# A Fourier filter and gated convolution on one core: taps over two blocks at once, transfers on one queue and in pieces, short products on zeros, and a new order of the work

## The chip, the cores and the metric

One NeuronCore of a Trainium2 chip runs the whole program. It has a matrix engine (PE, TensorE, with its weight loads shown apart as PEld), a vector engine (DVE), a scalar or activation engine (ACT), GpSimd (POOL) and a queue engine (SP, SyncE) that here only issues transfers. ACT can issue transfers as well. Data lie in HBM, in the on-chip SBUF of 128 partitions, and in PSUM, into which PE writes.

The metric is the time of one execution on the device in microseconds, from the median of several runs. A profile is of one execution; its span goes from its first to its last instruction.

## What is computed

The input x has 8 batches of 3200 positions and 256 channels. Per batch it is Fourier transformed along the positions, the spectrum is mixed by a complex 256 x 256 matrix with a bias, shrunk by 0.01 towards zero, and transformed back. On the result y a gate is formed from a causal convolution of five taps for each channel, multiplied with a 256 x 256 product of y, and multiplied by one more matrix.

```python
X = np.fft.rfft(x, axis=1)
Yr = Xr @ w_r - Xi @ w_i + b_r
Yi = Xr @ w_i + Xi @ w_r + b_i
Yr = np.sign(Yr) * np.maximum(np.abs(Yr) - lam, 0.0)      # Yi likewise, lam = 0.01
y = np.fft.irfft(Y, n=x.shape[1], axis=1)
...
for k in range(K):                                         # K = 5
    gate_pre += conv_w[k][None, None, :] * xp[:, k:k + S, :]
gate = 1.0 / (1.0 + np.exp(-gate_pre))
return (gate * (y @ w_val) @ w_out).astype(np.float32)
```

## The kernel before

3200 positions are split as 64 x 50, so that each transform is two stages of small matrix products. The stages of one batch are these:

- `p1`, units u = 0 to 7: load a unit of x (two halves of 50 rows, `load`), its products on PE (L553 to L560), a copy of one half of the result by ACT (L566), sum and difference on DVE (`fold`, L572), and a store of both to a scratch tensor `a_dram` in HBM (L514 by `by_rows`; the first unit has four odd stores of 25 rows, L592).
- `p2`, slices d = 0 to 6: load a slice of `a_dram` (L613), second transform on PE (L631), splitting of the result in a high and a low part on ACT and DVE (L672 to L684), mixing (`mixed`: `mix_sum` L749, bias on DVE L751, `mix` L745, shrinking L757 and L759), first inverse transform (L700), store to `z_dram` (L716).
- `positions`, blocks k = 0 to 7: load of `z_dram` (L800), second inverse transform (L811), copy to `y_sb` (L815). A block is 400 positions.
- `gated`, the same blocks: first product of the gate on ACT (`first`, L872), the four other taps on DVE (`tap`, L875), sigmoid on ACT (L885), the matrix product `v_ps` (L845, in the last batches L841), the gate on DVE (L887), a split in two parts (L348, L350), the matrix product `o_ps`, its copy (L912) and the stores of the output (L914). All of `first`, `tap` and sigmoid run per block and per half of the channels, over 400 elements in 128 partitions.

Matrices `w_val`, `w_out` and the taps arrive as 64-bit floats; `from_float64` turns one into 32-bit numbers by thirteen steps on DVE (L390, L396).

Several batches are under way at once. What is written in the program is not an order but pieces: each is given to `plan.add` with an engine, a due time `at`, its cost, and the tiles it uses and sets. `Plan.order` walks through a made timeline and, on each engine, takes of the pieces that can begin soonest the one with the smallest `at`; the numbers in the table `O` shift the due times of kinds of pieces. The engines then get their instructions in that order and work through them strictly in turn, waiting for tiles by semaphores. A tile of a pool with n buffers can be opened only when the one n before it has been read for the last time: PSUM has three buffers `ps_2` (for nearly everything) and two `ps_y` (for the mixing).

In batch 0 the halves of x and of the stores are spread over two queues, SP and ACT (`QUEUES`). For the first two batches loads of x and stores to `a_dram` are cut in pieces of 48 and 2 rows (`ROWS`); later they go as 50 rows. PE multiplies a tile of zeros between the early units (`warm`, L939), 8 of these products ahead of batch 1.

Of the kernel before, what the change touches and what calls it, by code (L numbers as in the profile page):

```python
# [10 lines left out]
F32 = mybir.dt.float32  # L11
# [10 lines left out]
NH = 2  # L22
# [82 lines left out]
class Plan:  # L105
# [30 lines left out]
    def order(self):  # L136
# [41 lines left out]
        while len(done) < len(pieces):  # L178
# [32 lines left out]
            p["start"], p["end"] = start, end  # L211
# [30 lines left out]
WIRE = 230  # L242
# [8 lines left out]
def act(n, kind="copy"):  # L251
# [9 lines left out]
O = {'spread': -43.2582,  # L261
     'hold': 0.1723,
     'together': 1.3472,
     'later': 16.9988,
     'load_x': -1.6525,
     'p1': -3.0866,
     'p1_step': 1.6595,
     'load_a': -5.4475,
     's2': -2.5217,
     's1i': 1.3927,  # L270
     'p3': 3.8457,
     'load_z': -27.5528,
     'y': 14.5177,
     'conv': 12.9924,
     'val': 3.2379,
     'gate': -21.5703,
     'project': 5.6082,
     'late_val': 6.023,
     'late_out': 14.484,
     'turn': -27.2503,  # L280
     'pre': 6.946,
     'mix_sum': -2.1531,
     'p1_1': -2.5925,
     'load_x_1': -0.3328,
     'p1_2': 0.3179,
     'p3_0': -1.1611}
# [9 lines left out]
def fourier_filter_then_gated_conv(ctx: ExitStack, tc: tile.TileContext, x, w_r, w_i, b_r, b_i,  # L296
# [224 lines left out]
    QUEUES = (("SP", nc.sync), ("ACT", nc.scalar))  # L521

    def p1(b, u, at):
# [55 lines left out]
        def store(h):  # L579
            if u == 0 and h in (0, None):  # L580
                buffer(ka, "a_dram", [Q, NM * D])
            dst = tl[ka].rearrange("(h f) mc -> f h mc", h=NH)
            hs = slice(0, NH) if h is None else slice(h, h + 1)
            eng = QUEUES[h][1] if early else nc.sync
            for k in range(2):
                lo = u * 4 * D + k * 512
                n = D if lo == 0 else 0
                by_rows(eng, dst[:, hs, lo + n:lo + 512], st()[k * HP:k * HP + N2, hs, n:], rows)
            if u == 0:
                for g in range(NH) if h is None else (h,):  # L590
                    for r in range(2):
                        eng.dma_start(out=dst[r::2, g, 0:D], in_=st()[r:N2:2, 1 - g if r else g, 0:D])  # L592
        for h in range(NH) if early else (None,):
            key = ("a_dram", b, (u, h))
            A_KEYS.setdefault(b, []).append(key)
            if early:
                STORED.append(("stored", 0, (u, h)))
            uses = [ks + (1,)] if h == 0 and u else [ks + (0,)] if h == 1 and u else [ks + (0,), ks + (1,)]
            add(at + 0.02, QUEUES[h][0] if early else "SP", 1300 if early else 1500, lambda h=h: store(h), uses,
                [key] + ([STORED[-1]] if early else []), {ka: "a_dram"} if u == 0 and not h else None, kb=200 if early else 400)  # L600
# [166 lines left out]
    AHEAD = 2  # L767
# [25 lines left out]
    def positions(b, k, at):  # L793
# [7 lines left out]
        add(at + O["load_z"], "SP", 400, load, [("z_dram", b, u) for u in range(NU)], [kz + (0,)], {kz: "zl"}, kb=400, chain="zl")  # L801
# [45 lines left out]

    def gated(b, k, at):
        bk = (b, k)
        here, there = y_keys(k, 0), [key for key in y_keys(k, 1) if key not in y_keys(k, 0)]  # L850
        ky, kg, kv, kh, kp, ko = (("y_hl", bk), ("acc", bk), ("v_ps", bk), ("gated", bk), ("o_ps", bk), ("o", bk))
# [14 lines left out]
        acc = lambda c: tl[kg][:, c, :]  # L866

        def first(c):
            if c == 0:
                buffer(kg, "acc", [P, 2 * TB])  # L870
                tl[kg] = tl[kg].rearrange("p (c n) -> p c n", c=2)
            nc.scalar.mul(block(acc(c)), y_at(k, c, 0), cw_sb[:, c, 0:1])  # L872

        def tap(c, j):
            nc.vector.scalar_tensor_tensor(out=block(acc(c)), in0=y_at(k, c, j), scalar=cw_sb[:, c, j:j + 1],  # L875
                                           in1=block(acc(c)), op0=ALU.mult, op1=ALU.add)
        for c in range(2):
            add(at + O["conv"] + 0.01 * c, "ACT", act(TB, "conv"), lambda c=c: first(c), [*here, *there, ("cw", 0, 0)],
                [kg + (c,)], {kg: "acc"} if c == 0 else None, chain="conv")
        for j in range(1, KC):  # L880
            for c in range(2):
                add(at + O["conv"] + 0.02 * j, "DVE", 61 + dve(TB), lambda c=c, j=j: tap(c, j), [*here, *there], [kg + (c,)],
                    delay=545 + (130 if j == KC - 1 else 0))
        for c in range(2):
            add(at + O["conv"] + 0.15, "ACT", act(TB, "sigmoid"), lambda c=c: nc.scalar.activation(  # L885
                out=acc(c), in_=acc(c), func=AF.Sigmoid), (), [kg + (c,)])
        add(at + O["gate"], "DVE", dve(2 * TB), lambda: nc.vector.tensor_tensor(  # L887
            out=tl[kg], in0=tl[kv][:, :, 0:TB], in1=tl[kg], op=ALU.mult), [kv + (0,), kv + (1,)], [kg + (0,), kg + (1,)])
        if bk in LATE_OUT:
            gs = [kg + (0,), ("w_late", 0, 0)]  # L890
            om = lambda e: matrix(kp, e, lambda: w_late[1], lambda h, c: tl[kg][:, c, :], True)
        else:
            gs = [*split(at + O["gate"] + 0.1, 2 * TB, kh, lambda: tl[kg], lambda: tl[kh][:, 0], lambda: tl[kh][:, 1],
                         [kg + (0,)], {kh: "g_hl"}, lambda: buffer(kh, "g_hl", [P, 2, 2, TB], F32R)),
# [38 lines left out]

    def warm(v, n):
# [5 lines left out]
    add(-200, "POOL", 100, lambda: nc.gpsimd.memset(nlam, -LAM), (), [("nlam", 0, 0)])  # L940

# [31 lines left out]
    for b in range(B):  # L973
# [13 lines left out]
        for k in range(NB + AHEAD):  # L987
            if k < NB:
                positions(b, k, start + (k - AHEAD) * T / NB)
            if k >= AHEAD:  # L990
                gated(b, k - AHEAD, start + (k - AHEAD) * T / NB)
    plan.run(tc)
# [25 lines left out]
```

## Time and profile before

| | |
|---|---|
| median of three runs | 868.22 us (866.73 to 869.12) |
| the profiled execution | 869.32 us, of which its span is 867.5 |
| PE busy | 825.7 us, 95% of the span |
| DVE busy | 768.2 us, 89% |
| ACT busy | 612.6 us, 71% |
| chain that ended last | PE 61%, DVE 16%, DMA 11%, ACT 6% |
| moved by DMA | 162.25 MB, mean 187 GB/s |

In what follows, L and a number is a line of the program before unless it is said to be of the changed one. A busy share is a mean over stages that have different limits; the tables by stage give busy time of each engine in a stretch with the number of its instructions, the TensorE clock that was granted (1.00 is full), the mean busy share of the 16 DMA engines, and GB/s. In a row of the timeline an idle time in brackets is that of the engine just before it, and what ended it. Rows of a long matrix product count each record of the profiler, of which a 32-bit product has two.

### The profile page before, as it was taken

What the parts mean: (1) busy time and instruction counts of PE and PEld (TensorE: products, weight loads), DVE (VectorE), ACT (ScalarE), POOL (GpSimd) and SP (SyncE); (2) the same over time, 40 slices, a digit from 0 to 9 for tenths busy, and PEclk for the clock granted to TensorE, in tenths of its full rate; (3) what the DMA queues carried; (4) which work ended last, traced back from release to release, by engine and by line L of the source; (5) the groups of instructions that cost most, each with busy time, mean ns of one, the idle gap of its engine ahead of it and who ended that gap; (6) DMA issues with size and microseconds to landing.
All of it is one profiled execution on the core that took longest, in us unless ns stands there. A gap on an engine that the chain in (4) does not pass through costs nothing.

```text
span 867.5 us, 23798 instructions
## 1 busy us (share of the span) xinstructions
PE 825.7 (95%) x9814; PEld 696.1 (80%) x9814; DVE 768.2 (89%) x1262; ACT 612.6 (71%) x1030; POOL 6.2 (1%) x11
## 2 busy tenths in 40 slices
PE   6888967999999999999999999999999999999997
PEld 2346755888888888898888898898888999998774
DVE  2526678799999999999999999999999999999996
ACT  1225645788877778787787778877787887776673
POOL 0000000000000000000000000000020000000000
PEclk7578989999999999999999999999999999999999
DMA  6679777768775668557675768557674557324422
GB/s 167 177 175 241 242 190 216 223 204 237 237 225 163 202 197 243 182 167 201 198 235 198 222 195 241 179 170 200 199 237 159 151 150 196 109 84 163 153 70 82
DMA packets 123973, 162.25 MB, mean 187 GB/s; under 512 B 10592, under 2 KB 98298, under 8 KB 123866
## 3 DMA queue, kind: packets, MB, share of 16 engines
q1 hardware_dynamic: 122106, 157.47, 61.3%
q10 hardware_dynamic: 1760, 3.28, 1.5%
q8 instruction: 77, 1.26, 0.6%
q14 instruction: 30, 0.25, 0.1%
HBM read 82.06 MB, written 78.64 MB: 185 GB/s over the span
## 4 chain that ended last, share of the span: by engine, by line
PE 61%; DVE 16%; DMA 11%; ACT 6%; issue 2%; SPq 2%; ACTq 0%; DVEq 0%
PE o_ps L845 12%; PE y_ps L745 11%; PE v_ps L845 10%; PE y_p L811 8%; PE y_ps L749 6%; DVE acc L875 5%; PE z_ps L700 4%; PE s L631 4%; DMA x<-in_x 3%; PE p L553 3%; DMA a<-a_dram 3%; DMA a_dram<-s 3%; DVE s L572 2%; DMA f_sb<-in_f 1%; DVE tp L759 1%
## 5 line engine op out<-in xcount | busy, mean ns | idle before, releaser
L875 DVE SCALAR_TENSOR_TENSOR acc<-y_sb,cw_sb,acc 128x400 f32<-128x400 f32 x512 | 301.5, 627 | 6.1 <-ACT acc L872 4.8
L745 PE MATMUL y_ps<-w_sb,xs 128*128 128x256 f32 x1152 | 156.9, 286 | 11.7 <-DVE y_ps L751 11.7
L745 PEld LDWEIGHTS y_ps<-w_sb,xs 128*128 128x128 f32 x1152 | 144.8, 190 | 22.3 <-DVE y_ps L751 13.7
L845 PE MATMUL o_ps<-gated,wo_sb 128*128 128x400 f32 x744 | 151.4, 349 | 0.7 <-DVE xs L680 0.4
L845 PEld LDWEIGHTS o_ps<-gated,wo_sb 128*128 128x128 f32 x744 | 132.4, 188 | 8.2 <-issue 2.5
L845 PE MATMUL v_ps<-y_hl,wv_sb 128*128 128x400 f32 x648 | 130.0, 347 | 1.4 <-ACT o L912 0.6
L572 DVE TENSOR_TENSOR s<-p,s 128x512 f32<-128x512 f32 (+2 forms) x144 | 89.9, 626 | 37.7 <-ACT s L568 22.6
L845 PEld LDWEIGHTS v_ps<-y_hl,wv_sb 128*128 128x128 f32 x648 | 115.5, 188 | 3.6 <-issue 1.3
L811 PEld LDWEIGHTS y_p<-g_sb,zl 100*64 100x64 f32 x2048 | 89.3, 137 | 26.0 <-issue 4.9
L811 PE MATMUL y_p<-g_sb,zl 100*64 100x100 f32 x2048 | 99.6, 252 | 0.5 <-issue 0.2
L749 PE MATMUL y_ps<-w_sb,xs 128*128 128x256 f32 x576 | 88.5, 292 | 6.0 <-ACT y_ps L727 5.5
L749 PEld LDWEIGHTS y_ps<-w_sb,xs 128*128 128x128 f32 x576 | 78.5, 193 | 16.0 <-ACT y_ps L727 11.3
L757 ACT ACTIVATE tp<-y_ps,nlam 128x512 f32<-128x512 f32 (+1 forms) x104 | 69.5, 672 | 24.3 <-PE y_ps L745 22.2
L872 ACT ACTIVATE acc<-y_sb,cw_sb 128x400 f32<-128x400 f32 x128 | 77.2, 630 | 12.0 <-DVE gated L350 11.9
L553 PE MATMUL p<-x,f_sb 50*64 50x512 f32 x256 | 71.2, 639 | 9.0 <-issue 6.3
L348 ACT CAST gated<-acc 128x800 fp32r<-128x800 f32 x62 | 53.4, 861 | 31.4 <-DVE acc L887 31.2
L759 DVE SCALAR_TENSOR_TENSOR tp<-y_ps,tp 128x512 f32<-128x512 f32 (+1 forms) x104 | 68.6, 663 | 5.8 <-ACT tp L757 5.4
L885 ACT ACTIVATE acc<-acc 128x400 f32<-128x400 f32 x128 | 66.9, 539 | 8.6 <-DVE acc L875 8.3
L560 PE MATMUL p<-x,f_sb 50*64 50x512 f32 x240 | 71.9, 646 | 0.0
L727 ACT COPY y_ps<-bias_sb 128x256 f32<-128x256 f32 x104 | 39.7, 382 | 45.5 <-DVE tp L759 38.5
L348 ACT CAST y_hl<-y_sb 128x800 fp32r<-128x800 f32 x54 | 46.5, 860 | 28.5 <-PE v_ps L845 26.5
L631 PEld LDWEIGHTS s<-f_sb,a 64*64 64x64 f32 x3072 | 52.1, 138 | 15.9 <-issue 6.8
(84 smaller groups left out, 1029.3 us busy)
## 6 DMA issues: line engine op xcount, KB each, us to landing
zl<-z_dram SPq DMA_DIRECT2D x64, 400.0 KB
out<-o SPq DMA_DIRECT2D x126, 200.0 KB
a<-a_dram SPq DMA_DIRECT2D x96, 256.0 KB
z_dram<-z_t SPq DMA_DIRECT2D x48, 512.0 KB
x<-in_x SPq DMA_DIRECT2D x90, 200.0 KB
a_dram<-s SPq DMA_DIRECT2D x90, 200.0 KB
x<-in_x SPq DMA_DIRECT2D x23, 192.0 KB
a_dram<-s SPq DMA_DIRECT2D x15, 192.0 KB
```

Source lines behind the costliest of these rows:

```text
L348: nc.scalar.copy(out=high(), in_=src())
L553: nc.tensor.matmul(p[k * HP:(k + 1) * HP, 0, :], f1_sb[half(0), 0:HP], xt[half(0), k * 512:(k + 1) * 512], start=True, stop=True)
L560: nc.tensor.matmul(dst, f1_sb[half(1), 0:HP], back[:, 2 * k:2 * k + 2, :], start=True, stop=True)
L572: nc.vector.tensor_tensor(out=st()[lo:hi, h, n], in0=tl[kp][lo:hi, 0, n], in1=st()[lo:hi, 1, n], op=(ALU.add, ALU.subtract)[h])
L631: nc.tensor.matmul(p[e * HP:(e + 1) * HP, h, c, t, :], tl[ka][rows, t, c * P + e * HP:c * P + (e + 1) * HP], f2_sb[rows, (4 * d + t) * N1: ...
L745: nc.tensor.matmul(p[:, 1 - r, :], xm(hx, c, r, i), w_sb[:, m, hw, c, :], start=False, stop=k == 5, skip_group_check=True)
L749: nc.tensor.matmul(tl[ky][:, 0], sm(hx, c, i), w_sb[:, 0, hw, c, :], start=False, stop=k == 5, skip_group_check=True)
L759: add(at + 0.2, "DVE", dve(n * D), lambda: nc.vector.scalar_tensor_tensor(out=tl[kt][:, 0:n], in0=tl[ky][:, 0:n], scalar=LAM, in1=tl[kt][: ...
L811: nc.tensor.matmul(dst[e * HP:(e + 1) * HP], zt[0:Q, m, c * P + e * HP:c * P + (e + 1) * HP], g, start=True, stop=True)
L845: nc.tensor.matmul(p[:, e, 0:TB], w[:, hw, c, e * P:(e + 1) * P], src(hy, c), start=n == 0, stop=n == 5)
L872: nc.scalar.mul(block(acc(c)), y_at(k, c, 0), cw_sb[:, c, 0:1])
L875: nc.vector.scalar_tensor_tensor(out=block(acc(c)), in0=y_at(k, c, j), scalar=cw_sb[:, c, j:j + 1], in1=block(acc(c)), op0=ALU.mult, op1=A ...
```

## The change

Five things are changed.

1. The gate's first product, taps and sigmoid run over two neighbouring blocks: a new function `conv` for each pair, over 800 elements instead of 400, so 256 taps for 512, 64 first products for 128 and 64 sigmoids for 128. The pair has one tile `acc`, twice as large. `gated` then takes its half of it. Positions run three blocks ahead of the gate instead of two.
2. In batch 0 only the second halves of the first two units of x are still loaded by ACT; all other loads and all stores go through SP, a store now taking both halves in one transfer. ACT runs a tiny copy as its first work.
3. Loads of x and stores to `a_dram` are cut in 48 and 2 rows in all batches; loads of `z_dram` in 96 and 4 rows.
4. `Plan.idle` looks for waits of PE in the made timeline between 36 and 200 us and `zeros` fills them with products of 128 x 128 zeros. That makes 26 products, ahead of three pieces.
5. The table `O` has new numbers, and some costs in the plan are new, so the order on every engine is another.

```diff
+    def idle(self, done):
...
+            places = [(since, t) for t, since in opened.items() if since < until <= first[t]]
+            if "ps_2" in p["new"].values():
+                places.append((p["open"], None))
+            since, t = min(places, key=lambda q: q[0], default=(until, None))
+            n = int(0.8 * (until - max(at, since) - 300) / 214)
+            if n > 1:
+                yield p["n"], t, n
...
+FILL = 36000, 200000
-WIRE = 230
+WIRE = 250
...
-O = {'spread': -43.2582,
+O = {'spread': -91.8948,
...
+    def zeros(p, n, start):
+        for j in range(n):
+            nc.tensor.matmul(p[:, 0, 0:P], zero_sb, zero_sb, start=start, stop=start, skip_group_check=not start)
...
-        rows = ROWS if b < 2 else ((0, N2),)
+        rows = ROWS
...
-                eng = QUEUES[g][1] if early else nc.sync
+                eng = QUEUES[g][1] if early and u < BOTH else nc.sync
...
-        def store(h):
+        def store():
...
-            eng = QUEUES[h][1] if early else nc.sync
...
-                by_rows(eng, dst[:, hs, lo + n:lo + 512], st()[k * HP:k * HP + N2, hs, n:], rows)
+                by_rows(nc.sync, dst[:, :, lo + n:lo + 512], st()[k * HP:k * HP + N2, :, n:], rows)
...
-    AHEAD = 2
+    AHEAD = 3
...
-            nc.sync.dma_start(out=zt[0:Q], in_=tl["z_dram", b][:, k * MB * D:(k + 1) * MB * D])
+            by_rows(nc.sync, zt, tl["z_dram", b][:, k * MB * D:(k + 1) * MB * D], ((0, 96), (96, Q)))
...
+    def conv(b, kk, at):
+        k = 2 * kk
...
+        wide = lambda c, j: pair(y_sb, (MB * k + j) * N2, (N1 - 2 * MB - 2 * MB * k) * N2, w)[:, c]
...
+            nc.scalar.mul(acc(c), wide(c, 0), cw_sb[:, c, 0:1])
...
+            nc.vector.scalar_tensor_tensor(out=acc(c), in0=wide(c, j), scalar=cw_sb[:, c, j:j + 1], in1=acc(c), op0=ALU.mult, op1=ALU.add)
...
         add(at + O["gate"], "DVE", dve(2 * TB), lambda: nc.vector.tensor_tensor(
-            out=tl[kg], in0=tl[kv][:, :, 0:TB], in1=tl[kg], op=ALU.mult), [kv + (0,), kv + (1,)], [kg + (0,), kg + (1,)])
+            out=part(), in0=by_half(tl[kv][:, :, 0:TB]), in1=part(), op=ALU.mult), [kv + (0,), kv + (1,)], ours)
...
+    add(-199, "ACT", 1300, lambda: nc.scalar.copy(out=b_sb[HP:HP + 1, 0:1], in_=tl[ki][HP:HP + 1, 0:1]), [ki + (0,)], [("b", 0, 2)])
```

What this does to the order is shown at three places. First ACT in batch 0, before: a copy of a unit's products (`s1` from `p1`), then stores of the unit before it.

```order
L566 COPY s1_203<-p1_182 128x512
L514 DMA a_dram_164<-s1_173 48x512
L514 DMA a_dram_164<-s1_173 2x512
L566 COPY s1_219<-p1_196 128x512
L514 DMA a_dram_164<-s1_203 48x512
L514 DMA a_dram_164<-s1_203 2x512
L566 COPY s1_233<-p1_214 128x512
```

And ACT at the same place in the changed program, where the loads of the second unit are its last transfers:

```order
L554 DMA x_100<-in_x 2x1024
L607 COPY s1_148<-p1_129 128x512
L609 COPY s1_148<-p1_129 64x256
L607 COPY s1_162<-p1_140 128x512
L607 COPY s1_177<-p1_155 128x512
L607 COPY s1_196<-p1_181 128x512
```

The copies of ACT stand one behind another; nothing that it issues stands between them.

Second SP's queue where the last store of batch 0 is followed by loads (`g1`, a constant; `x`, units of batch 1; `a`, slices of batch 0). Before:

```order
L514 DMA a_dram_164<-s1_267 2x512
L450 DMA g1_sb_70<-in_g1 128x256
L514 DMA x_322<-in_x 48x1024
L514 DMA x_322<-in_x 2x1024
L514 DMA x_322<-in_x 48x768
L514 DMA x_322<-in_x 2x768
L514 DMA x_322<-in_x 48x256
L514 DMA x_322<-in_x 2x256
L514 DMA x_329<-in_x 48x1024
L514 DMA x_329<-in_x 2x1024
L613 DMA a_334<-a_dram_164 64x4x256 x2
```

SP in the changed program:

```order
L554 DMA a_dram_168<-s1_254 2x2x512
L490 DMA g1_sb_70<-in_g1 128x256
L650 DMA a_293<-a_dram_168 64x4x256 x2
L554 DMA x_296<-in_x 48x1024
L554 DMA x_296<-in_x 2x1024
L554 DMA x_296<-in_x 48x768
L554 DMA x_296<-in_x 2x768
L554 DMA x_296<-in_x 48x256
L554 DMA x_296<-in_x 2x256
L650 DMA a_303<-a_dram_168 64x4x256 x2
```

The first slice now stands ahead of the loads of x, and one unit of x stands between the first slice and the second.

Third DVE at the end of the program, from the gate of the sixth block of the last batch on (`acc` from `v_ps` is a gate, `acc` from `y_sb` a tap, `gated` a low part). Before:

```order
L887 TENSOR_TENSOR acc_10801<-v_ps_10824,acc_10801 128x800
L875 SCALAR_TENSOR_TENSOR acc_10836<-y_sb_77,cw_sb_75,acc_10836 128x400 x3
L350 TENSOR_TENSOR gated_10866<-acc_10801,gated_10866 128x800
L875 SCALAR_TENSOR_TENSOR acc_10836<-y_sb_77,cw_sb_75,acc_10836 128x400 x3
L875 SCALAR_TENSOR_TENSOR acc_10879<-y_sb_77,cw_sb_75,acc_10879 128x400 x2
L887 TENSOR_TENSOR acc_10836<-v_ps_10860,acc_10836 128x800
L875 SCALAR_TENSOR_TENSOR acc_10879<-y_sb_77,cw_sb_75,acc_10879 128x400 x6
L887 TENSOR_TENSOR acc_10879<-v_ps_10875,acc_10879 128x800
```

DVE at the end of the changed program:

```order
L933 TENSOR_TENSOR acc_10605<-v_ps_10663,acc_10605 128x2x400
L899 SCALAR_TENSOR_TENSOR acc_10667<-y_sb_78,cw_sb_75,acc_10667 128x800
L390 TENSOR_TENSOR gated_10683<-acc_10605,gated_10683 128x800
L899 SCALAR_TENSOR_TENSOR acc_10667<-y_sb_78,cw_sb_75,acc_10667 128x800
L390 TENSOR_TENSOR gated_10703<-acc_10605,gated_10703 128x800
L899 SCALAR_TENSOR_TENSOR acc_10667<-y_sb_78,cw_sb_75,acc_10667 128x800 x4
L933 TENSOR_TENSOR acc_10667<-v_ps_10700,acc_10667 128x2x2x200
L933 TENSOR_TENSOR acc_10667<-v_ps_10754,acc_10667 128x2x400
```

Before, the gate of the seventh block stood ahead of the last six taps of the eighth; now all taps of the last pair stand ahead of both of its gates.

More of the change, by code (lines that the diff above doesn't have):

```diff
@@ L227, in order, with run @@
         return done
-    def run(self, tc):
+    def idle(self, done):
+        opened, first = {}, {}
+        for p in done:
+            for t in p["tiles"]:
+                if t[0] == "y_ps":
+                    if t in p["new"]:
+                        opened[t] = p["end"]
+                    elif p["engine"] == "PE":
+                        first.setdefault(t, p["start"])
+        free = 0.0
+        for p in done:
+            if p["engine"] != "PE":
+                continue
+            at, until = free, p["start"]
+            free = p["start"] + p["busy"]
+            if not FILL[0] < until < FILL[1]:
+                continue
+            places = [(since, t) for t, since in opened.items() if since < until <= first[t]]
[5 more added lines that the diff above has]
+                yield p["n"], t, n
+    def run(self, tc, fill=None):
+        done = self.order()
+        more = {n: (t, m) for n, t, m in self.idle(done)} if fill else {}
         with tc.manual_schedule():
-            for p in self.order():
+            for p in done:
+                if p["n"] in more:
+                    fill(*more[p["n"]])
                 p["fn"]()
@@ L846, in matrix, with first, tap @@
                 n += 1
+    def conv(b, kk, at):
+        k = 2 * kk
+        here = sorted({*y_keys(k, 1), *y_keys(k + 1, 1)})
+        kg = ("acc", (b, kk))
+        w = 2 * MB * N2
+        acc = lambda c: tl[kg][:, c]
+        wide = lambda c, j: pair(y_sb, (MB * k + j) * N2, (N1 - 2 * MB - 2 * MB * k) * N2, w)[:, c]
+        def first(c):
+            if c == 0:
+                tl[kg] = room(kg, "acc", 4 * TB).rearrange("p (c h n) -> p c h n", c=2, h=NH)
+            nc.scalar.mul(acc(c), wide(c, 0), cw_sb[:, c, 0:1])
+        def tap(c, j):
+            nc.vector.scalar_tensor_tensor(out=acc(c), in0=wide(c, j), scalar=cw_sb[:, c, j:j + 1], in1=acc(c), op0=ALU.mult, op1=ALU.add)
+        for c in range(2):
+            add(at + O["conv"] + 0.01 * c, "ACT", act(2 * TB, "conv"), lambda c=c: first(c), [*here, ("cw", 0, 0)],
+                [kg + (c, e) for e in range(2)], {kg: "acc"} if c == 0 else None, chain="conv")
+        for j in range(1, KC):
+            for c in range(2):
+                add(at + O["conv"] + 0.02 * j, "DVE", 61 + dve(2 * TB), lambda c=c, j=j: tap(c, j), here,
+                    [kg + (c, e) for e in range(2)],
+                    delay=961 + (130 if j == KC - 1 else 0))
+        for c in range(2):
+            add(at + O["conv"] + 0.15, "ACT", act(2 * TB, "sigmoid"), lambda c=c: nc.scalar.activation(
+                out=acc(c), in_=acc(c), func=AF.Sigmoid), (), [kg + (c, e) for e in range(2)])
     def gated(b, k, at):
         bk = (b, k)
[L850 to L851 removed]
+        here = y_keys(k, 0)
+        ky, kg, kv, kh, kp, ko = (("y_hl", bk), ("acc", (b, k // 2)), ("v_ps", bk), ("gated", bk), ("o_ps", bk), ("o", bk))
         if bk in LATE_VAL:
@@ L863, in gated @@
                 {kv: "ps_2"} if e == 0 else None, chain="val")
[L866 to L886, printed above, removed]
+        ours = [kg + (c, k % 2) for c in range(2)]
@@ L989, in fourier_filter_then_gated_conv, with fill @@
                 positions(b, k, start + (k - AHEAD) * T / NB)
-            if k >= AHEAD:
-                gated(b, k - AHEAD, start + (k - AHEAD) * T / NB)
-    plan.run(tc)
+            if k >= AHEAD and k % 2:
+                i = k - AHEAD
+                conv(b, i // 2, start + i * T / NB)
+                for j in range(2):
+                    gated(b, i + j, start + (i + j) * T / NB)
+    def fill(t, n):
+        if t is None:
+            ahead.append(n)
+        else:
+            zeros(tl[t], n, False)
+    plan.run(tc, fill)
 _INS = ["x", "w_r", "w_i", "b_r", "b_i", "moe_w_val", "moe_conv_w", "moe_w_out"]
```

93 lines of the change are left out of this document (49 added, 44 removed).

## The prediction

> **What bounds the kernel now.** I read the page's head, then busy time by stage, then the chain and single stretches of the timeline.
>
> ```profile
> span 867.5 us, 23798 instructions
> 0.00:42.00 42.00, 32.24 (x94) 12.02 (x95) 15.72 (x26) 9.17 (x16) 1.15 (x9) 0.68 0.65 172
> 42.00:80.00 38.00, 32.49 (x333) 21.32 (x332) 16.26 (x26) 13.30 (x23) 0.00 (x0) 0.77 0.85 194
> 80.00:112.00 32.00, 28.18 (x411) 22.33 (x410) 21.25 (x36) 19.72 (x36) 0.00 (x0) 1.00 0.85 251
> ...
> 120.00:160.00 40.00, 32.68 (x524) 27.27 (x525) 31.60 (x63) 22.53 (x40) 0.00 (x0) 0.94 0.72 189
> 160.00:400.00 240.00, 237.86 (x3098) 207.04 (x3093) 231.59 (x381) 191.04 (x322) 0.00 (x0) 1.00 0.68 210
> 400.00:640.00 240.00, 238.12 (x3011) 211.41 (x3011) 232.47 (x378) 187.91 (x319) 0.00 (x0) 1.00 0.67 203
> 640.00:840.00 200.00, 200.00 (x2253) 178.82 (x2252) 192.02 (x307) 154.09 (x256) 5.01 (x2) 1.00 0.48 144
> 840.00:867.00 27.00, 21.30 (x80) 14.32 (x78) 19.72 (x32) 12.30 (x20) 0.00 (x0) 0.97 0.28 91
> ```
>
> Each row gives start and end, length, then busy time of PE, weight loads, DVE, ACT and POOL, then PE's granted clock, the DMA share and GB/s. From 160 to 840 us PE is idle for 680 - 675.98 = 4.0 us: that stage is bound by PE, at full clock, and DVE (656 of 680) is busy beside it without ending PE's waits. A cheaper DVE stage can therefore win at most those 4 us there. Before 160 PE waits, and its busy time includes warming products and half clock: the start is where time can be had. After 840 it waits again.
>
> **The start.** These rows are from the chain (the first), the timeline (start, length, engine, line, count) and once more busy time by stage; a q marks an engine's issuing of DMAs.
>
> ```profile
> 16.23 3.61 DMA x<-in_x
> ...
> 24.63 1.42 DVE L572 TENSOR_TENSOR s<-p,s 128x512 f32<-128x512 f32 x2 [4.78 <-ACT s L566]
> ...
> 29.27 0.59 ACT L566 COPY s<-p 128x512 f32<-128x512 f32 x1 [2.27 <-DMA a_dram<-s]
> ...
> 30.09 1.33 ACTq L514 DMA_DIRECT2D a_dram<-s  x4
> 31.61 0.59 ACT L566 COPY s<-p 128x512 f32<-128x512 f32 x1 [1.76 <-DMA a_dram<-s]
> ...
> 18.40 2.17 ACTq L514 DMA_DIRECT2D a_dram<-s  x4
> ...
> 21.08 1.48 SPq L592 DMA_DIRECT2D a_dram<-s  x2
> ...
> 26.78 14.88 SPq L514 DMA_DIRECT2D a_dram<-s  x24
> 41.70 0.36 SPq L450 DMA_DIRECT2D g_sb<-in_g  x1
> 42.16 3.86 SPq L514 DMA_DIRECT2D x<-in_x  x10
> 46.06 1.34 SPq L613 DMA_DIRECT2D a<-a_dram  x2
> ...
> 51.13 1.15 PE L631 MATMUL s<-f_sb,a 64*64 64x64 f32 x60 [0.85 <-DMA a<-a_dram]
> ...
> 60.00:65.00 5.00, 5.00 (x58) 3.50 (x57) 0.72 (x2) 1.32 (x2) 0.00 (x0) 0.68 0.41 100
> ...
> 64.96 1.30 SPq L613 DMA_DIRECT2D a<-a_dram  x2
> ...
> 95.55 1.50 SPq L613 DMA_DIRECT2D a<-a_dram  x2
> ```
>
> In the chain x of batch 0 loads until 16.23 + 3.61 = 19.8 us, one transfer behind another; the same bytes go in the same pieces after the change, so this stays. Stores begin at 18.4. Now ACT copies a unit, waits for DVE, issues four stores itself and only then copies the next: copies at 29.27 and 31.61 are 2.34 us apart, each ended by the issue before it, though four issues take 1.33 and a copy 0.59. SP's 24 stores of units 2 to 7 last 14.88, or 0.62 each, where an issue alone costs 1.33 / 4 = 0.33.
>
> After the change ACT issues none of them. Step by step, for SP: unit 0 has 4 plain stores and the 4 odd ones (1.48 for two): 4 x 0.33 + 2 x 1.48 = 4.3, from 18.6 to 22.9; unit 1 another 1.3, to 24.2; three constants 1.4 (what they take now), to 25.6. Up to there nothing is won, since SP now carries both halves. Units 2 to 7 are 24 issues with twice the bytes: 24 x 0.33 = 7.9 is the least; their 2.46 MB (100 rows of 4 KB a unit, six units) at the 194 GB/s of the second row take 12.7, at the 251 of the third 9.8. I take 11.4: end at 37.0, where it is 41.66 now. The next load, a of batch 0, reads those stores, so the last must land: 1.8 us estimated (0.5 at least; 5.1, which the first a load takes from 46.06 to 51.13 under load, at most). It then goes out at 38.8, not 46.06: **7.3 us earlier**, 4 of them by not standing behind ten loads of x. Where ACT's cover goes, the DVE folds are next, 1.42 a unit, which is less than 11.4 / 6 = 1.9.
>
> Next the order of loads. Before the third a load now stand 2.4 MB from the first on (2 x 0.52 of a, 3 x 0.41 of x, 0.13): 12.4 us at 194 GB/s, so 51.2 instead of 64.96. That lead shrinks, for the bytes ahead of the last a load are the same but for one x of 0.41 MB (2.1 us at 194, 1.6 at 251). The stream starts at 38.8 where its first x load is now at 42.16: 3.4 + 1.6 to 2.1, so the last a load leads by 5 us, by up to 8 if the hole from 60 to 65, where the DMA share is 0.41, closes too. Middle 6.
>
> Then comes DVE's conversion of the first matrix, which the change leaves as it is:
>
> ```profile
> 112.22 2.18 DVE L390 TENSOR_SCALAR st<-st 128x512 int32<-128x512 int32 x5
> ...
> 119.06 0.43 DVE L751 TENSOR_TENSOR y_ps<-y_ps,bias_sb 128x256 f32<-128x256 f32 x1
> ...
> 119.55 2.93 PE L745 MATMUL y_ps<-w_sb,xs 128*128 128x256 f32 x12 [5.16 <-DVE y_ps L751]
> ```
>
> PE stands 5.16 us behind eleven steps, and in the new order the same sum stands behind the same eleven steps: nothing won, nothing lost. For the second matrix the new order has two x products, a slice's transform and two mixes free meanwhile; that covers about 1 us of PE's wait (0 to 3). **Start: 6 + 1 = 7 us** (3 to 11).
>
> **Products on zeros.** There are only 26: 15 before the first transform, 9 and 2 later.
>
> ```profile
> L623 PE MATMUL s<-f_sb,a 128*128 128x128 f32 x32 | 5.0, 277 | 0.0
> ...
> 35.00:40.00 5.00, 5.00 (x10) 2.65 (x9) 4.79 (x8) 3.01 (x7) 0.00 (x0) 0.50 0.71 175
> ...
> 55.00:60.00 5.00, 3.47 (x42) 2.81 (x41) 1.43 (x3) 0.20 (x1) 0.00 (x0) 0.50 0.88 169
> ```
>
> Products of that shape, 16 in 32 records, take 5.0 us, so one 0.31 and the first 15 some 4.7. They lie in a wait of PE (warming ends near 37, the data come near 43), which hides them; if the data come early they cost up to 3. The clock is at half with PE fully busy, and at half again after waits, so a clock kept up could shorten the first mixes by some 3 us, if they were then the bound. I take 0 and keep -3 to +3. The Trainium skill (TensorE: Matmul & The Clock Gate, Part 1: The HAM clock gate) has full clock only after about 3.4 us of sustained work in a free-running window; by that the 15 products keep a clock that the warming products have raised, if the wait behind them is short, and win those 3 us; if not, nothing. The row for 35 to 40 differs: PE counts as busy throughout and the clock stayed at half.
>
> **Taps over two blocks.**
>
> ```profile
> L875 DVE SCALAR_TENSOR_TENSOR acc<-y_sb,cw_sb,acc 128x400 f32<-128x400 f32 x512 | 301.5, 627 | 6.1 <-ACT acc L872 4.8
> L679 DVE TENSOR_TENSOR sx<-s,sx 128x512 f32<-128x512 f32 x48 | 33.0, 688 | 25.3 <-ACT xs L676 20.3 <-PE y_ps L745 3.6 <-ACT sx L672 1.4
> L680 DVE TENSOR_TENSOR xs<-s,xs 128x1024 fp32r<-128x1024 f32 x48 | 58.4, 1216 | 0.1
> ...
> 831.90 4.36 DVE acc L875 x8
> ```
>
> In a run of eight a tap costs 4.36 / 8 = 0.545. The slope is (1216 - 688) / 512 = 1.03 ns an element, so a tap of 800 takes 0.545 + 0.41 = 0.96. DVE saves 512 x 0.545 - 256 x 0.96 = 33 us, 5 us a batch; ACT's first products and sigmoids save their fixed part too. All of it lies beside PE from 160 on. What it can give is part of the 4.0 us of idle PE; I take **2** (0 to 4). New wait: the first gate of a pair now stands behind eight wide taps, 7.7 us, instead of 4.4; behind it on DVE are subtractions that PE's output products need. PE's other work covers that, since mixes and positions stand between.
>
> **The tail.**
>
> ```profile
> 857.79 1.08 ACT L885 ACTIVATE acc<-acc 128x400 f32<-128x400 f32 x2 [2.61 <-DVE acc L875]
> 858.91 0.99 DVE L887 TENSOR_TENSOR acc<-v_ps,acc 128x800 f32<-128x800 f32 x1 [0.60 <-ACT acc L885]
> ...
> 820.69 2.69 PE v_ps L841 x8
> 823.38 2.19 PE o_ps L845 x12
> ...
> 859.96 2.95 PE L841 MATMUL o_ps<-acc,w_late 128*128 128x400 f32 x8 [1.61 <-DVE acc L887]
> ```
>
> PE's last wait is 1.61. In the new order PE has o_ps and v_ps (2.2 + 2.7 = 4.9, the two rows of the chain) while DVE has four wide taps (3.8), ACT a wide sigmoid (0.95, estimated as 0.54 and the slope above) and DVE the gate (0.99): 5.8. The wait is about 1 instead of 1.6, but both gates come at the end: **0** (-2 to +1).
>
> **Sum.** The profiled execution took 869.3 (span and 1.8 around it); 7 + 2 + 0 = 9 less is 860.3. It lies 1.1 above the median of 868.2, so **859.2** as a median. Summed ends: 3 + 0 - 1 - 3 would be 1 slower, 11 + 4 + 2 + 3 would be 848.
>
> **Rivals.** (1) One queue stores no faster than two: units 2 to 7 still need 14.9 us. Then the a load waits until 42.3; only not standing behind x is won, and later loads catch up with the old order: 2 for the start, 2 after it, **864**. For it: the DMA share is 0.65 there already. Against: 0.62 an issue, and ACT's waits for its own issues. (2) The stores go at the issue's pace, the second conversion is covered and PE's idle vanishes: 11 + 4, **853**. (3) Slower: SP's queue. By the program's order it issues 1003 transfers where it had 727, because x, stores and zl go in two pieces in every batch. Each loaded block of y and each a slice stands in line behind them; at a batch's turn PE has mixes only if a has landed. If each of the seven turns waits 2 us, 14 - 9 makes it **873**; it decides from 1.3 us a turn. Against: 276 more at 0.33 are 91 us over 868, and at 160 to 640 the queue has room, the DMA share being 0.68. The Trainium skill (DMA: Bandwidth & Descriptors, Rules for kernel authors) advises against two transfers to disjoint partitions, as they share the same engines; by that the pieces bring nothing and cost their issue. The same page (Why a DMA increments its semaphore by 16 and not by 1) lets 50 rows use 10 engines and 48 use 16, which would make the pieces pay; no row here shows the engines of one transfer. (4) The change doesn't do what it says: PE's order is as full of waits, start included, **868**.
>
> **How the numbers follow.** Forecast 0.60 (855 to 863), rival 1 0.14, 2 0.13, 3 0.07, 4 0.06. The range from 850 to 867 leaves out rival 3, half of 4 and the outer part of 2. A difference under 0.3% (2.6 us) can't be told from none. Faster takes the forecast, 2 and most of 1: 0.83; same takes 4 and the rest of 1: 0.10; slower 0.07.
>
> **What would show it.** The first a load at 37 to 41 us, and the first transform's products some 8 us before 51.13; PE without gaps from about 153; taps of 0.96 and DVE near 735 us in all; idle PE of 2 between there and the last blocks. I am wrong if the stores of units 2 to 7 still take 14 us, if PE's waits for DMA show up at batch turns, or if the conversions keep PE waiting longer than now.

## The result, and the profile after

| | before | changed |
|---|---|---|
| median | 867.81 us (866.73 to 869.12, 4 runs) | 857.50 us (856.26 to 859.73, 4 runs) |
| profiled execution, span | 869.32 us, 867.5 | 859.73 us, 857.8 |
| PE, DVE, ACT busy | 825.7, 768.2, 612.6 | 821.0, 736.2, 593.7 |

The ratio is 0.988 (95% interval 0.9865 to 0.9896): **10 us faster**, where 859.2 was predicted. The total holds. The sum of 7 at the start, 2 from the taps and 0 at the tail does not: as the rest shows, it was 0 to 3 at the start, about 10 in the long middle, where wide taps, pieces of z and the order are needed together, and 0 at the tail. All medians and ranges here are of runs in the fast state; one slow run, of whole_zl, is not counted.

First busy time by stage of the changed kernel, with the columns known from before (start and end, length, busy PE, weight loads, DVE, ACT, POOL, then clock, DMA share, GB/s).

```profile
42.00:80.00 38.00, 30.11 (x382) 21.04 (x383) 16.50 (x27) 13.21 (x22) 0.00 (x0) 0.82 0.84 198
...
112.00:120.00 8.00, 3.78 (x17) 3.78 (x18) 5.98 (x13) 2.10 (x4) 0.00 (x0) 0.50 0.63 154
120.00:160.00 40.00, 34.92 (x578) 28.13 (x579) 31.39 (x63) 24.89 (x43) 0.00 (x0) 0.94 0.90 249
160.00:400.00 240.00, 238.23 (x3090) 213.46 (x3083) 228.39 (x305) 187.60 (x286) 0.00 (x0) 1.00 0.74 201
400.00:640.00 240.00, 239.97 (x3130) 215.17 (x3128) 225.82 (x305) 187.06 (x286) 0.00 (x0) 1.00 0.77 209
640.00:840.00 200.00, 198.75 (x2151) 175.41 (x2144) 181.81 (x224) 145.53 (x208) 3.26 (x2) 1.00 0.47 138
```

From 160 to 840 us PE is idle for 680 - 676.95 = 3.05 us, before 4.0: by that, the stage won 1 us. But PE did more in the same time: in the 240 us from 400 on 3128 weight loads instead of 3011.

The start, in the timeline of the changed kernel (start, length, engine, line, count; in brackets the idle time before a row and what ended it):

```profile
26.42 11.80 SPq L554 DMA_DIRECT2D a_dram<-s  x24
38.27 0.36 SPq L490 DMA_DIRECT2D g_sb<-in_g  x1
40.99 1.33 SPq L650 DMA_DIRECT2D a<-a_dram  x2
...
46.03 1.87 PE L668 MATMUL s<-f_sb,a 64*64 64x64 f32 x58 [0.79 <-DMA a<-a_dram]
...
51.83 1.36 SPq L650 DMA_DIRECT2D a<-a_dram  x2
...
91.43 1.89 SPq L650 DMA_DIRECT2D a<-a_dram  x2
...
116.22 2.93 PE L782 MATMUL y_ps<-w_sb,xs 128*128 128x256 f32 x12 [7.65 <-DVE y_ps L788]
...
142.53 2.93 PE L786 MATMUL y_ps<-w_sb,xs 128*128 128x256 f32 x12 [4.47 <-ACT y_ps L764]
```

The stores end at 38.2 (predicted 37.0), the first slice is asked for at 40.99 (38.8), the third at 51.83 (51.2), and the last at 91.43, 4.1 us ahead of before (6). The first transform's products begin 5.1 us earlier than the old 51.13. But behind the first conversion PE now stands 7.65 us instead of 5.16, and behind the second 4.47 instead of 2.78. Both times the twelve records after the wait run in 2.93; before, they did so behind the first conversion only, and behind the second took 1.68:

```profile
146.81 1.68 PE L745 MATMUL y_ps<-w_sb,xs 128*128 128x256 f32 x12 [2.78 <-DVE y_ps L751]
```

The granted clock is 0.58 from 142 to 146 us in the changed kernel, and 1.00 from 146 to 150 before.

**How far each kernel leads.** Stages are interleaved in another order now, so that no single product marks the same point in both. For the table below each product of the trace counts with the distance to the next that is usual for its kind (118 ns for a record of the mix, 183 for one of `v_ps` or `o_ps`, 336 in the last batches, 110 for `p`, 60 for `z_ps`, 47 for `y_p`, 15 for `s`; zeros and warming count nothing). The sum is 750.2 us for every kernel. A row gives how much later than before (less is earlier) the sum passes 60, 140, 300, 500 and 660 us, and the span ends; before it does so at 135, 225, 393, 602, 769 and 867.5 us. The names are those of the experiments.

| kernel | 60 | 140 | 300 | 500 | 660 | end |
|---|---|---|---|---|---|---|
| changed | -2.5 | -0.2 | -3.9 | -7.8 | -10.1 | -9.7 |
| again (the changed kernel, second profile) | -3.7 | -0.5 | -4.7 | -8.8 | -11.1 | -10.7 |
| no_zeros | -5.2 | -2.6 | -6.4 | -10.6 | -12.9 | -12.6 |
| short_conv | -5.8 | -5.1 | -9.4 | -13.6 | -15.7 | -15.4 |
| narrow_taps | -3.9 | -0.1 | -1.3 | -0.2 | 0.8 | 6.1 |
| narrow | -4.9 | 1.1 | 0.0 | 0.2 | 1.0 | 5.2 |
| whole_rows | -3.9 | -1.6 | -3.3 | 2.6 | 3.8 | 4.1 |
| whole_zl | -3.7 | -0.8 | -2.1 | -4.5 | -4.9 | -4.5 |
| woven3 | -3.1 | 0.8 | -3.6 | -7.8 | -9.9 | -9.6 |
| two_queues | 9.8 | 6.2 | 8.5 | 6.2 | 4.1 | 4.6 |
| old_numbers | -3.5 | 4.3 | 4.7 | 6.7 | 7.0 | 7.3 |
| before_early | -4.9 | -4.9 | -4.9 | -4.9 | -5.0 | -5.0 |
| before_pieces | -1.2 | 0.4 | 0.5 | 0.7 | 2.1 | 3.5 |

At 225 us nothing or little is left of the start's lead: 0.2, 0.5 and 2.6 us in three profiles with the changed kernel's order and start. From there to 769 us PE wins 9.9, 10.6 and 10.3. A second count says where these come from. Of the products between 160 and 820 us that have a semaphore to wait for, those whose last signal came after the product ahead of them had begun stood beyond the usual distance by 23.1 us together before, and by 12.0 and 10.9 in the two profiles of the changed kernel. Most of it is short waits in which the view shows PE as busy, for the idle time shown fell by 1 us only.

### The profile page after: what moved, and what is told of

Read it like the earlier page. It is cut to its first block, busy times and chain, and to the rows that moved or that the text cites. A ratio compares the mean times of both kernels' runs of the same rounds, so it can differ in the third digit from the quotient of the medians.

```text
span 857.8 us, 23810 instructions
## 1 busy us (share of the span) xinstructions
PE 821.0 (96%) x9866; PEld 700.7 (82%) x9866; DVE 736.2 (86%) x1006; ACT 593.7 (69%) x903; POOL 4.5 (1%) x12
## 4 chain that ended last, share of the span: by engine, by line
PE 69%; DVE 13%; DMA 9%; ACT 4%; SPq 3%; issue 2%; DVEq 0%; ACTq 0%
PE o_ps L882 13%; PE y_ps L782 12%; PE v_ps L882 11%; PE y_p L848 10%; PE y_ps L786 6%; DMA x<-in_x 4%; PE p L594 4%; PE s L668 4%; PE z_ps L737 4%; DVE acc L899 4%; PE v_ps L878 2%; SPq L554 2%; DMA zl<-z_dram 1%; DVE acc L933 1%; DVE gated L390 1%
## 5 line engine op out<-in xcount | busy, mean ns | idle before, releaser
L899 DVE SCALAR_TENSOR_TENSOR acc<-y_sb,cw_sb,acc 128x800 f32<-128x800 f32 x256 | 263.0, 1047 | 16.1 <-ACT acc L896 15.6
L782 PE MATMUL y_ps<-w_sb,xs 128*128 128x256 f32 x1152 | 156.3, 286 | 11.1 <-DVE y_ps L788 11.0
L882 PEld LDWEIGHTS o_ps<-gated,wo_sb 128*128 128x128 f32 x744 | 134.6, 188 | 4.1 <-DVE gated L390 1.1
L848 PE MATMUL y_p<-g_sb,zl 100*64 100x100 f32 x2048 | 97.4, 251 | 0.7 <-DMA zl<-z_dram 0.5
L933 DVE TENSOR_TENSOR acc<-v_ps,acc 128x800 f32<-128x800 f32 x64 | 62.9, 984 | 11.4 <-PE v_ps L878 5.5
L909 ACT ACTIVATE acc<-acc 128x800 f32<-128x800 f32 x64 | 55.8, 878 | 16.3 <-DVE acc L899 16.0
L958 ACT COPY o<-o_ps 128x800 f32<-128x800 f32 x63 | 51.8, 822 | 21.3 <-PE o_ps L882 15.8
L716 DVE TENSOR_TENSOR sx<-s,sx 128x512 f32<-128x512 f32 x48 | 33.0, 688 | 38.2 <-ACT xs L713 37.2
```

Of the source, the lines that this page charges most:

```text
L782: nc.tensor.matmul(p[:, 1 - r, :], xm(hx, c, r, i), w_sb[:, m, hw, c, :], start=False, stop=k == 5, skip_group_check=True)
L848: nc.tensor.matmul(dst[e * HP:(e + 1) * HP], zt[0:Q, m, c * P + e * HP:c * P + (e + 1) * HP], g, start=True, stop=True)
L882: nc.tensor.matmul(p[:, e, 0:TB], w[:, hw, c, e * P:(e + 1) * P], src(hy, c), start=n == 0, stop=n == 5)
L899: nc.vector.scalar_tensor_tensor(out=acc(c), in0=wide(c, j), scalar=cw_sb[:, c, j:j + 1], in1=acc(c), op0=ALU.mult, op1=ALU.add)
```

## The experiments

Theory A is the prediction (start 7, taps 2). Theory B came from the table: the taps' relief of DVE is worth 9 to 10 between 225 and 769 us, and the start's lead is lost at the conversions. Medians and ratios come from the timed runs; spans, waits and the table from one profile each, so a point of the table moves by 1 to 3 us with the start.

**Narrow taps.** Two kernels with the changed order on every engine. In the first, every wide instruction of the gate becomes two at the same place:

```diff
-            nc.scalar.mul(acc(c), wide(c, 0), cw_sb[:, c, 0:1])
+            for h in range(NH):
+                nc.scalar.mul(acc(c)[:, h], wide(c, 0)[:, h], cw_sb[:, c, 0:1])
...
-            nc.vector.scalar_tensor_tensor(out=acc(c), in0=wide(c, j), scalar=cw_sb[:, c, j:j + 1], in1=acc(c), op0=ALU.mult, op1=ALU.add)
+            for h in range(NH):
+                nc.vector.scalar_tensor_tensor(out=acc(c)[:, h], in0=wide(c, j)[:, h], scalar=cw_sb[:, c, j:j + 1], in1=acc(c)[:, h], op0=ALU.mult, op1=ALU.add)
```

and the sigmoid likewise. In the second only the taps are.

> The changed kernel, where each wide first product, tap and sigmoid is two instructions of 400 elements instead of one of 800, at the same place; the order on every engine stays as it is. DVE gets 256 x (2 x 0.545 - 0.96) = 33 us more, ACT some 64 + 64 fixed parts more. Theory A (the prediction: the start is worth 7 us, taps 2): at most 2 to 4 us slower than the changed kernel, 860 to 862. Theory B (from the comparison of the two traces: PE's lead grows by 1 to 2 us in every batch from 225 us on, out of short waits for DVE and ACT that count as busy PE): 6 to 9 us slower, 864 to 867.

> The changed kernel, where only the taps on DVE are two instructions of 400 elements; first products and sigmoids on ACT stay wide; the order stays. With taps, first products and sigmoids narrow it took 873.0. If DVE's 33 us are what PE felt: 868 to 873. If ACT's fixed parts are: 857 to 861. If the two add: 863 to 867.

Measured 873.01 us (871.37 to 874.67; ratio to before 1.0064, 1.0044 to 1.0083) and 876.08 (874.03 to 877.99; 1.0098, 1.0082 to 1.0114): 15.5 and 18.6 slower than the changed kernel, more than either theory gave and, for narrow_taps, above all three values that were expected. With ACT's instructions narrow too the kernel isn't slower, so ACT's wide ones bring nothing that can be seen; DVE's do. The taps' rows, of the changed kernel and then of narrow_taps (group, busy time, mean ns, idle time before):

```profile
L899 DVE SCALAR_TENSOR_TENSOR acc<-y_sb,cw_sb,acc 128x800 f32<-128x800 f32 x256 | 263.0, 1047 | 16.1 <-ACT acc L896 15.6
```

```profile
L900 DVE SCALAR_TENSOR_TENSOR acc<-y_sb,cw_sb,acc 128x400 f32<-128x400 f32 x512 | 294.8, 628 | 13.4 <-ACT acc L896 13.3
```

DVE differs by 31.8 us. Now the stretch from 225 to 769 us in three kernels: before, changed, narrow_taps.

```profile
225.00:769.00 544.00, 540.69 (x6905) 482.43 (x6895) 528.97 (x856) 429.62 (x725) 5.01 (x2) 1.00 0.63 191
```

```profile
225.00:769.00 544.00, 543.04 (x6949) 491.99 (x6948) 512.49 (x681) 422.54 (x640) 3.26 (x2) 1.00 0.70 194
```

```profile
225.00:769.00 544.00, 536.52 (x6871) 480.45 (x6871) 523.22 (x851) 412.70 (x625) 3.40 (x2) 1.00 0.70 193
```

PE is shown idle for 3.3, 1.0 and 7.5 us. Its weight loads tell more: 482, 492 and 480 us of them in the same 544. With narrow taps and the new order PE does no more than before, and in the table the kernel keeps the pace of before (-0.1 at the mark of 140, 0.8 at 660), where the changed one wins 10. Short waits, counted as above, are 22.1 us again. So with this order the wide taps are worth 11 us there, and the idle time of 3.3 us shown before was no bound. The rest of the loss, 5 us by the table, is behind 769 us: in the new order all taps of the last pair stand ahead of both gates. The waits of narrow_taps from 840 us on (what waited for what: us, times, longest) make up 2.7 of it; the rest is not shown.

```profile
PE v_ps L878 <- DVE acc L934: 1.1, 1, 1.1
PE o_ps L882 <- DVE gated L390: 0.9, 1, 0.9
PE o_ps L882 <- ACT o L959: 0.7, 1, 0.7
```

**Whole rows.** Again the changed order, with the pieces taken back: for x and stores from the third batch on and for `z_dram` in one kernel, for `z_dram` alone in the other.

```diff
-            by_rows(nc.sync, zt, tl["z_dram", b][:, k * MB * D:(k + 1) * MB * D], ((0, 96), (96, Q)))
+            nc.sync.dma_start(out=zt[0:Q], in_=tl["z_dram", b][:, k * MB * D:(k + 1) * MB * D])
...
-        rows = ROWS
+        rows = ROWS if b < 2 else ((0, N2),)
```

> The changed kernel, where from the third batch on x and the stores to a_dram go as 50 rows, and blocks of z_dram as 100 rows in all batches; the order stays, SP issues 276 or so transfers less. Theories A and B: within 1 us of the changed kernel, since PE does not wait for DMA there (idle PE from 160 to 840 us is 3 us). Rival 3 (SP's queue is late): 2 to 4 us faster. If the pieces pay by landing sooner: 2 to 4 us slower.

> The changed kernel, where only the blocks of z_dram are loaded as 100 rows again; x and stores keep their pieces; the order stays. If the block's own transfer lands later when it is whole: all of the loss of the run with whole rows comes back, 868 to 873, with PE waiting for zl by 5 us or more in all. If x and the stores as 50 rows held the queue up: within 2 us of the changed kernel, 856 to 860.

Measured 872.89 us (866.82 to 878.32; ratio 1.0055, 1.0028 to 1.0083) and 866.41 (861.99 to 872.35; 0.9985, 0.9963 to 1.0007): 15 and 9 slower than the changed kernel, and spread more. The theories were wrong, rival 3 more so: fewer transfers cost time. Whole blocks of z bring 9 of the 15, so neither expectation for whole_zl holds in full; x and stores as 50 rows bring the other 6. PE's waits from 160 to 840 us, in whole_rows, in whole_zl, and in the changed kernel:

```profile
PE y_p L848 <- DMA zl<-z_dram: 10.8, 8, 4.1
```

```profile
PE y_p L848 <- DMA zl<-z_dram: 3.9, 7, 1.2
```

```profile
PE y_p L848 <- DMA zl<-z_dram: 0.5, 1, 0.5
```

Loaded whole, blocks of z come late for PE. The other way round, the kernel before got the pieces, by the same two lines turned round and with its order kept:

> The kernel before, where x and the stores to a_dram go as 48 and 2 rows in all batches and blocks of z_dram as 96 and 4 rows; the order on every engine stays. If pieces pay by themselves (as undoing them in the changed kernel cost 15 us): 860 to 864. If they pay only where the order loads a block late, as the changed one does: within 2 us of before, 866 to 870, since PE of before waits for no block of z there. If SP's queue suffers from 276 more issues: 870 to 875.

869.79 us (867.96 to 873.05; ratio 1.0013, 0.9999 to 1.0027): no difference. No wait of PE for a block of z is shown before from 160 to 840 us, so there is nothing to win. The pieces are not a gain but a condition of the new order, which needs z sooner: from the issue of a block's load to the first product on it pass 15.8 us before and 8.1 in the changed kernel (medians of 64 blocks).

**Zeros.**

```diff
-    plan.run(tc, fill)
+    plan.run(tc)
```

> The changed kernel without the 26 products on zeros; nothing else moves. Theories A and B: within 1 us. If the zeros keep the clock up: up to 3 us slower; if they only take time: 1 us faster.

857.03 us (856.95 to 860.34; ratio 0.9891, 0.9871 to 0.9912), the changed kernel's time. Rows by stage, changed kernel and no_zeros:

```profile
35.00:40.00 5.00, 5.00 (x33) 3.81 (x32) 0.00 (x0) 0.75 (x2) 0.00 (x0) 1.00 0.76 205
...
55.00:60.00 5.00, 5.00 (x97) 4.05 (x98) 2.70 (x6) 2.09 (x4) 0.00 (x0) 1.00 0.82 183
```

```profile
35.00:40.00 5.00, 0.00 (x0) 0.00 (x0) 0.00 (x0) 0.00 (x0) 0.00 (x0) 0.68 0.75 213
...
55.00:60.00 5.00, 5.00 (x79) 3.45 (x79) 1.59 (x3) 0.51 (x2) 0.00 (x0) 0.50 0.79 175
```

The zeros do hold the clock: 1.00 for 0.50 around 57 us. That wins no time. The likely reason, which no run shows by itself, is that PE waits for data and for DVE at several places behind. The lead of no_zeros in the table is the start of its one profile: it is there at 94 us, and the medians don't show it.

**Early transfers.** In the changed kernel loads and stores of batch 0 were spread over SP and ACT again, with the old `store(h)`; in the kernel before they were put on SP, with the new `store()`. The planner makes a new order in both.

```diff
-    BOTH = 2
+    BOTH = 8
```

```diff
-                eng = QUEUES[g][1] if early else nc.sync
+                eng = QUEUES[g][1] if early and u < 2 else nc.sync
```

> The changed kernel, where loads of x and stores of batch 0 are spread over SP and ACT again, in halves, as before; the planner orders anew. Theory A: the start's 7 us are gone, 863 to 865. Theory B: the conversions on DVE near 110 and 135 us hold PE up until about the same time in either case, so 0 to 2 us slower, 857 to 860.

> The kernel before with the second part of the change alone: all stores of batch 0 and all but two second halves of its loads go through SP, a store taking both halves; the planner orders anew with the numbers of before. If the early transfers bring the start's 7 us by themselves: 860 to 863. If they bring the 2 us or so by which the changed kernel leads at 140 to 225 us: 865 to 867. If they need the new numbers, as all other parts did: 868 to 880.

Measured 875.77 us (873.12 to 880.21; ratio 1.0103, 1.0076 to 1.013) and 864.49 (862.49 to 867.21; 0.9972, 0.9958 to 0.9987). The first is 18 slower than the changed kernel, outside both expectations, 12.3 of it by the mark of 60; what the part costs and what its order costs can't be told apart in it. The second tells: the part alone, with the old numbers, brings 2.3 us of the median. Between the two profiles it is 5.0, but the profiled execution of before is 1.5 us above its median. In its table row -4.9 stays -4.9 from 135 us to the end. In before_early the last of the stores ends at 38.07 and the first slice is asked for at 43.56:

```profile
29.91 8.16 SPq L514 DMA_DIRECT2D a_dram<-s  x18
38.11 0.36 SPq L450 DMA_DIRECT2D g_sb<-in_g  x1
43.56 1.35 SPq L609 DMA_DIRECT2D a<-a_dram  x2
```

**The conversions.** Two kernels with the changed order but for DVE's steps at the conversions. In one the thirteen steps are woven between what stands behind them. In the other, which leaves out most of the conversion and so gives no valid output, eleven of them are shortened (here those of two inputs):

```diff
+        for p in done:
+            if p["n"] in mine:
+                kept.append(p)
+                continue
...
+            out.append(p)
+            if kept and p["engine"] == "DVE":
+                emit(3)
```

```diff
-                nc.vector.tensor_tensor(out=w[out], in0=w[in0], in1=w[in1], op=op_)
+                m = slice(0, n if n < 100 else 8)
+                nc.vector.tensor_tensor(out=w[out][:, m], in0=w[in0][:, m], in1=w[in1][:, m], op=op_)
```

> The changed kernel, where the thirteen steps of each of the two large conversions are woven, three at a time, between the steps of DVE that stand behind them, so that a sum for the mixing waits for three steps at most; nothing else moves. The changed kernel's PE waits 7.65 us there at 116 us and 4.47 at 142. If PE's work bounds all that follows: 6 to 9 us faster than the changed kernel, 849 to 852. If a lead at the start is lost again in the second batch (both kernels had done the same work at 225 us, though the changed one led by 4.5 at 70): within 2 us, 856 to 860.

> The changed kernel, where eleven of the thirteen steps of each of the two large conversions work on 8 of 512 elements, so that most of w_val and w_out is not converted; every instruction stays in its place. Each conversion is some 4.5 us shorter on DVE. If PE's work bounds all that follows, so that a lead won at the start is kept: PE's waits of 7.65 and 4.47 us shrink by 4.5 and 3 to 4.5, and the end comes 7 to 9 us earlier, 848 to 851. If a lead won at the start is lost again behind 160 us: 855 to 858.

woven3 took 858.78 us (856.7 to 860.99; ratio 0.9888, 0.9866 to 0.991), no gain, for PE's wait only moved, to the next sum and the next bias copy:

```profile
108.60 1.68 PE L807 MATMUL y_ps<-w_sb,xs 128*128 128x256 f32 x12 [0.83 <-DVE y_ps L813]
...
118.27 2.93 PE L807 MATMUL y_ps<-w_sb,xs 128*128 128x256 f32 x12 [5.28 <-DVE y_ps L813]
...
142.94 2.93 PE L811 MATMUL y_ps<-w_sb,xs 128*128 128x256 f32 x12 [5.45 <-ACT y_ps L789]
```

It can't tell whether a lead is kept. short_conv took 854.27 us (853.19 to 856.49; ratio 0.985, 0.9834 to 0.9865), 3.2 less than the changed kernel by the medians, 5.7 by the two spans. That lies between its two expectations. PE's waits there:

```profile
110.09 2.93 PE L784 MATMUL y_ps<-w_sb,xs 128*128 128x256 f32 x12 [3.78 <-DVE y_ps L790]
...
137.64 2.93 PE L788 MATMUL y_ps<-w_sb,xs 128*128 128x256 f32 x12 [2.42 <-ACT y_ps L766]
```

They are shorter by 3.9 and 2.05, together 5.9, but that is not what was won. PE's order is the same in both kernels here, so the same product can be looked up in both traces. Just ahead of the first conversion short_conv already leads the changed kernel's profile by 2.3 us, behind the second by 4.9, and at the end by 5.7. So the shorter conversions brought 2.6 of it, near the 3.2 of the medians; most of the rest is the start, which varies. Within one order, what leads at 160 us is kept to 1 us.

Is the changed kernel's lead lost at the conversions, then? The same count as in the table above, at the sums of 35, 75 and 140 us, which the kernel before passes at 94, 156 and 225 us, that is ahead of both conversions, behind both, and later:

| kernel | 35 | 75 | 140 |
|---|---|---|---|
| changed | -2.0 | -0.8 | -0.2 |
| again | -4.5 | -1.2 | -0.5 |
| no_zeros | -6.2 | -3.5 | -2.6 |
| short_conv | -5.8 | -5.7 | -5.1 |
| before_early | -4.9 | -4.9 | -4.9 |

With the changed order 1.2 to 3.3 us are lost between 94 and 156 us, and 0.6 to 0.9 more up to 225; with short conversions 0.1 and 0.6. But the conversions are no fixed barrier. DVE begins the first at 112.22 us before, at 108.92 in the changed kernel and at 107.36 in before_early, and there a lead of 4.9 passes both of them whole, with the waits of the old order:

```profile
114.66 2.93 PE L741 MATMUL y_ps<-w_sb,xs 128*128 128x256 f32 x12 [5.13 <-DVE y_ps L747]
...
141.94 1.68 PE L741 MATMUL y_ps<-w_sb,xs 128*128 128x256 f32 x12 [2.78 <-DVE y_ps L747]
```

So the loss comes from the order that the changed kernel has around them. In the first profile of the changed kernel, part of the lead was gone ahead of them: 2.0 us are left at 94 us, where the other two have 4.5 and 6.2.

**The numbers.** The changed kernel with the table `O` and the rate `WIRE` of before (two of the lines):

```diff
-WIRE = 250
+WIRE = 230
...
-O = {'spread': -91.8948,
+O = {'spread': -43.2582,
```

> The changed kernel with the table O and the rate WIRE of before, so with wide taps, pieces, SP's early transfers and zeros in another order. If the order is what fits the durations of the changed parts: 866 to 876. If the parts bring their gain in any order: 856 to 861.

877.02 us (876.83 to 877.07; ratio 1.0097, 1.0076 to 1.0117): all parts of the change together, in the order that the old numbers make of them, are 9 us slower than none. By its row of the table it is 4.3 us behind at 229 us, and 3 more at the end.

**The changed kernel again.**

> The changed kernel once more, for a second profile of it. Time 856 to 859. In the kernels with its order and start the wait for the first slice a came out between 4 and 9 us: if the start varies by itself, this profile's lead over before at 140 to 225 us differs from the first one's by 1 to 3 us; if not, by less than 0.5.

858.26 us (856.29 to 858.74; ratio 0.9895, 0.9879 to 0.9912). Its lead differs from the first profile's by 2.5 us at the sum of 35, by 1.2 at 60 and by 0.3 at 140: the start does vary, and most of that is gone by 225 us. No kernel here that does all of the work is faster than the changed one by more than the runs spread. The tiny copy on ACT and the positions running three blocks ahead were not taken back by themselves.

## Why the prediction was right, and where it was not

- **The stores and the first loads: right.** 11.80 us for 11.4, the third slice at 51.83 for 51.2. The landing ahead of the first slice was put too short: from 38.22 to 40.99 it is 2.8, not 1.8 (inside the bounds of 0.5 and 5.1), so the first slice won 5.1 us and not 7.3, and the last slice leads by 4.1, not by 6. One reading does not hold: the rows of ACT's copies name the landing of stores (`DMA a_dram<-s`) as what ended their waits, not ACT's issuing, and two such waits, of 1.32 and 1.67 us, remain in the changed kernel, where ACT issues no store.
- **The conversions: wrong, and this step failed at the start.** "Nothing won, nothing lost" for the first and "covers about 1 us" for the second make a gain of 1; measured is a loss of 1.2 to 3.3 between 94 and 156 us. The first wait is 2.5 us longer, since PE had reached the sum with less other work left, while the thirteen steps (eleven in the prediction) still stood in front; two waits of 2.10 and 1.19 us near 130 us, which only the old order has, make up for some of it. The second is 4.47 us instead of 2.78, behind the copy of the bias into a buffer that is read by a step behind the conversion, and what follows it runs at half clock. In the old order (before_early) the same conversions cost no lead. Start: 0 to 3 for the 7 forecast.
- **Zeros: right, 0.** The rule cited (the Trainium skill, TensorE: Matmul & The Clock Gate, Part 1: The HAM clock gate) agrees with the rows behind the zeros, 1.00 for 0.50. The row that the prediction set against it, 35 to 40 us of before, busy throughout at 0.50, is not explained by any run. The 3 us that a warm clock might have won did not come (857.03 without the zeros, 857.50 with them).
- **Taps: right in the duration, wrong in the worth.** A wide tap was put at 0.96 us and DVE at 735; DVE is busy 736.2 us (a tap's mean is 1.047 with its overlap, as the narrow one's was 0.627 where it took 0.545). But "a cheaper DVE stage can therefore win at most those 4 us there" took PE's shown idle time as the bound of what PE loses. PE won 10 between 225 and 769 us, and narrow taps took all of it away. The term of 2 should have been 10, most of it out of short waits that stand in no idle column; whole blocks of z take more than half of it away too (4.1 won instead of 9.9), so it is not the taps' alone.
- **Tail: right within its bounds.** PE's wait of 1.61 ahead of the last `o_ps` is gone, and the lead changes from 10.1 at 769 us to 9.7 at the end.
- **Rival 3: the reverse.** SP's queue bears the pieces; without them PE waits 10.8 us for z. The Trainium skill (DMA: Bandwidth & Descriptors, Rules for kernel authors) advises against two transfers to disjoint partition halves; for these uneven pieces, in this order, that advice does not hold. The Trainium skill (DMA: Bandwidth & Descriptors, Why a DMA increments its semaphore by 16 and not by 1) lets 96 rows use 16 engines and 100 only 10, which would explain it, but no row here shows the engines of one transfer.

Two errors of opposite sign, 4 to 7 us too much at the start and 8 too little behind it, made the total right by luck. What the order itself brings apart from wide taps stays open: the taps' worth was measured in the new order only, and by old_numbers they may bring nothing in another.

## What to carry to other kernels

An engine at 99% busy in the profile can still lose 3% to short waits; count what it gets done between two marks, its weight loads for instance, before taking its idle time as the most that can be won beside it. A lead at the start has to be followed through the order that will run: in the old order 4.9 us passed both conversions whole, in the new one 1 to 3 us were lost there. And two traces of the same order should be compared product by product before a difference of their ends is put down to one change: 2.3 of the 5.7 us between short_conv and the changed kernel were there before the changed steps. In a kernel whose order is fixed ahead, parts are not additive: wide taps and pieces, each taken back in the new order, and early transfers, taken back with an order made anew, cost 15 to 19 us here out of a gain of 10, so price a part in the order that it will run in.

## What the runs showed of the hardware that was not expected

- Of one PE-bound stage of 660 us before, 23 us were short waits, nearly all for DVE and ACT, with 4.0 us shown as idle from 160 to 840.
- A block of z as 96 and 4 rows instead of 100 made the kernel 9 us faster in one order (866.41 to 857.50), and pieces made no difference in the other (ratio 1.0013).
- In before_early a lead is kept to 0.1 us from 94 us to the end: 4.9 to 5.0.
- Zeros held PE's clock at 1.00 instead of 0.50 and the time did not move (857.03 and 857.50).
